# Moving eight modulation matrix products out of the QKV stage, and reworking the normalization of the attention readout, in an adaLN + linear attention + GEGLU block

## The chip, the cores and the metric

The kernel runs on one core of a Trainium2 chip. The metric is the device time of one execution in microseconds (us); lower is better. A core has a matrix engine (TensorE, "PE" in the profile; "PEld" is its weight load), a vector engine (VectorE, "DVE"), a scalar engine (ScalarE, "ACT"), GpSimd ("POOL") and a queue engine that issues DMAs (SyncE, "SP"). TensorE writes its results to tiles in a memory called PSUM. A tile of 128x512 float32 is called one bank here; a tile of 128x1024, such as `k_ps` below, is counted as two. The operands and all other tiles on the core are in a second memory, SBUF.

TensorE's clock is granted by hardware: the profile shows it as a share of full speed (over the whole execution 0.970 in the kernel before). A kernel of one core has no second die to compare with, so a run counts as fast unless it is over 1.5% above the fastest of the same kernel.

## The reference, cut to what matters

```python
# x [1, 2048, 1024], wqkv [1024, 3072], wo [1024, 1024], c [1, 1024], w_mod [1024, 6144]
# w_gate, w_up [1024, 3584], w_down [3584, 1024]; all bf16; 32 heads of 32
mod = silu(c) @ w_mod                       # six vectors of 1024: sa, ca, ga, sb, cb, gb
h = layernorm(x) * (1 + ca) + sa
q, k, v = split_heads(h @ wqkv)
phi(t) = where(t > 0, t + 1, exp(t)) + 1e-6
kv  = phi(k)^T v          (per head, 32x32)
den = phi(q) . sum_s phi(k) + 1e-6
num = phi(q) kv
x = x + ga * ((num / den) @ wo)             # linear attention
h = layernorm(x) * (1 + cb) + sb
x = x + gb * ((gelu(h @ w_gate) * (h @ w_up)) @ w_down)
```

## The kernel before

The 6144 columns of `w_mod` are treated as 12 blocks of 512. One block costs a 1 MB load, 8 matmuls of 128x512, a copy, and for four of the six vectors 4 transposes. Blocks 0 to 3 (`sa`, `ca`) are needed before the first q; the other eight only after the attention. Before the change those eight sit inside the QKV loop, one after each group of q, because TensorE has work to hide them under:

```python
    def mod_block(blk, scratch, apsum, small):
        ...
        wmb = scratch[blk % 2]
        nc.sync.dma_start(out=wmb, in_=w_mod_v[:, :, blk * NCH:(blk + 1) * NCH])
        ps = apsum.tile([P, NCH], FP32, name="mod_ps", tag="modps")
        for kt in range(KD):
            nc.tensor.matmul(ps[:], lhsT=silu_bc[:, kt, :], rhs=wmb[:, kt, :],
                             start=(kt == 0), stop=(kt == KD - 1))
        # ... evict; for sa, ca, sb, cb also 4 transposes ("mod_pst") and copies ...

    # QKV stage, for each of 4 blocks tb of 512 tokens:
                for g in range(G):
                    ps = cps_q.tile([P, NCH], FP32, name="q_ps")
                    # ... 8 matmuls, phi ...
                    if tb < 2:
                        for _ in range(a2_per_g):
                            if a2_blocks:
                                mod_block(a2_blocks.pop(0), scratch_A2, apsum2, small2)
                # ... last tb: load wo, multiply it by ga_bc on VectorE ...
                for tt in range(4):
                    psk = cps_kv.tile([P, D], FP32, name="k_ps")     # two banks
                    psv = cps_kv.tile([P, D], FP32, name="v_ps")     # two banks
                    # ... 16 + 16 matmuls, phi on k, copy of v ...
```

After QKV come `kv` (128 matmuls of 128x129) and the denominators `den` (32 matmuls). The reciprocal `rbf` has one row for each head and block of tokens (4 x 32 = 128 rows). To divide `num` by it, the 32 rows of the block of tokens are spread over 128 partitions by a matmul with a 0/1 matrix `esel4`, which uses 32 rows of the array:

```python
        for tb in range(TB):
            for g in range(G):
                psn = c4ps.tile([P, NCH], FP32, name="num_ps")
                nc.tensor.matmul(psn[:], lhsT=kvbd[:, g, :], rhs=pqT[:, g, tb * NCH:(tb + 1) * NCH],
                                 start=True, stop=True)
                pse = c4ps.tile([P, NCH], FP32, name="rexp_ps")
                nc.tensor.matmul(pse[:], lhsT=esel4[tb * H:(tb + 1) * H, g, :], rhs=rbf[tb * H:(tb + 1) * H, :],
                                 start=True, stop=True, tile_position=(tb * H, 0))
                rexp = c4w.tile([P, NCH], BF16, name="rexp")
                nc.scalar.activation(out=rexp[:], in_=pse[:], func=ACT.Identity)
                nc.vector.tensor_tensor(out=oT[:, g, tb * NCH:(tb + 1) * NCH], in0=psn[:], in1=rexp[:],
                                        op=ALU.mult)
```

Then the output projection with the second layernorm (`att_ps`, the normalized `h2t`, 128 transposes `ln_pt`, evicted to `HTbuf` by ScalarE), and the FFN: gate `g_ps`, up `u_ps`, down `d_ps`, 896 matmuls each. `gb` is applied by multiplying `w_down` with `gb_bc` as it arrives, 28 pieces of 128x1024.

Of the kernel before, what the change touches and what calls it, by code (L numbers as in the profile page):

```python
# [12 lines left out]
P = 128  # L13
# [6 lines left out]
def kernel(  # L20
# [41 lines left out]
    nc.vector.memset(eps_den[:], 1e-6)  # L62
    sa_col = consts.tile([P, KD], FP32, name="sa_col")
# [7 lines left out]
    HTbuf = longp.tile([P, max(KD * S, 2 * KD * NCH)], BF16, name="HTbuf")  # L71
# [3 lines left out]
    PKbuf = longp.tile([P, max(T * D, 8 * D + 2 * KD * NCH)], BF16, name="PKbuf")  # L75
# [20 lines left out]
    def mod_scratch(buf, base):  # L96
        return [buf[:, base + i * KD * NCH: base + (i + 1) * KD * NCH].rearrange("p (k n) -> p k n", k=KD)
                for i in range(2)]
    scratch_A1 = mod_scratch(HTbuf, 0)
    scratch_A2 = mod_scratch(PKbuf, 8 * D)  # L100

# [7 lines left out]
    def mod_block(blk, scratch, apsum, small):  # L109
        vec = (blk * NCH) // D  # L110
        off = (blk * NCH) % D
        wmb = scratch[blk % 2]
        nc.sync.dma_start(out=wmb, in_=w_mod_v[:, :, blk * NCH:(blk + 1) * NCH])
        ps = apsum.tile([P, NCH], FP32, name="mod_ps", tag="modps")
        for kt in range(KD):
            nc.tensor.matmul(ps[:], lhsT=silu_bc[:, kt, :], rhs=wmb[:, kt, :],
                             start=(kt == 0), stop=(kt == KD - 1))
        if vec in (2, 5):
            dst = ga_bc if vec == 2 else gb_bc
            nc.vector.tensor_copy(out=dst[:, off:off + NCH], in_=ps[:])  # L120
        else:
            modrow = small.tile([P, NCH], BF16, name="modrow")
            nc.scalar.activation(out=modrow[:], in_=ps[:], func=ACT.Identity)
            pst = apsum.tile([P, 4, P], BF16, name="mod_pst", tag="modps")
            for j in range(4):
                nc.tensor.transpose(out=pst[:, j, :], in_=modrow[:, j * P:(j + 1) * P],
                                    identity=ident[:])
            cidx = off // P
            if vec == 0:
                nc.vector.tensor_copy(out=sa_col[:, cidx:cidx + 4], in_=pst[:, :, 0])  # L130
            elif vec == 3:
                nc.vector.tensor_copy(out=sb_col[:, cidx:cidx + 4], in_=pst[:, :, 0])
            else:
                tmp = small.tile([P, 4], BF16, name="onep_tmp")
                nc.vector.tensor_scalar(out=tmp[:], in0=pst[:, :, 0], scalar1=1.0, scalar2=None,
                                        op0=ALU.add)
                dst = onepca_col if vec == 1 else onepcb_col
                nc.vector.tensor_copy(out=dst[:, cidx:cidx + 4], in_=tmp[:])
# [7 lines left out]
    with ExitStack() as pa:  # L146
# [5 lines left out]
        x_pre = []  # L152
        for t in range(4):
            xt = lnw.tile([P, D], BF16, name="xt")
            nc.sync.dma_start(out=xt[:], in_=x2d[t * P:(t + 1) * P, :])
            x_pre.append(xt)

        with tc.tile_pool(name="apsum1", bufs=1, space=bass.MemoryType.PSUM) as apsum1:
# [4 lines left out]
            nc.sync.dma_start(out=crow, in_=c)  # L163
            nc.scalar.activation(out=sig_row, in_=crow, func=ACT.Sigmoid)
# [7 lines left out]
            with tc.tile_pool(name="apsum1b", bufs=2, space=bass.MemoryType.PSUM) as apsum1b:  # L172
                for blk in range(0, 4):
                    mod_block(blk, scratch_A1, apsum1b, small2)
# [4 lines left out]
        with ExitStack() as pc:  # L179
            lnps = pc.enter_context(tc.tile_pool(name="lnps1", bufs=1, space=bass.MemoryType.PSUM))  # L180
            cps_q = pc.enter_context(tc.tile_pool(name="cps_q", bufs=2, space=bass.MemoryType.PSUM))
            cps_kv = pc.enter_context(tc.tile_pool(name="cps_kv", bufs=1, space=bass.MemoryType.PSUM))
            apsum2 = pc.enter_context(tc.tile_pool(name="apsum2", bufs=1, space=bass.MemoryType.PSUM))
            nc.gpsimd.memset(v_ext[:, :, :, P:P + 1], 1.0)
            a2_blocks = list(range(4, (6 * D) // NCH))
            a2_per_g = -(-len(a2_blocks) // (min(TB, 2) * G))
            for tb in range(TB):
# [28 lines left out]
# [3 lines that stand above are left out]
                        nc.tensor.matmul(ps[:], lhsT=wqkv_v[:, kt, g * P:(g + 1) * P],  # L219
                                         rhs=hT[:, kt, tb * NCH:(tb + 1) * NCH],  # L220
                                         start=(kt == 0), stop=(kt == KD - 1))
                    phi_evac(cwork, ps[:], pqT[:, g, tb * NCH:(tb + 1) * NCH], NCH, "q")
                    if tb < 2:
                        for _ in range(a2_per_g):
                            if a2_blocks:
                                mod_block(a2_blocks.pop(0), scratch_A2, apsum2, small2)
                if tb == TB - 1:
                    for kt in range(KD):
                        nc.sync.dma_start(out=wo_v[:, kt, :], in_=wo_dram[:, kt, :])
                        nc.vector.tensor_tensor(out=wo_v[:, kt, :], in0=wo_v[:, kt, :], in1=ga_bc[:], op=ALU.mult)  # L230
                for tt in range(4):
                    t = tb * 4 + tt
                    psk = cps_kv.tile([P, D], FP32, name="k_ps")
                    psv = cps_kv.tile([P, D], FP32, name="v_ps")
                    for nh in range(2):
                        for kt in range(KD):
                            nc.tensor.matmul(psk[:, nh * NCH:(nh + 1) * NCH], lhsT=hT[:, kt, t * P:(t + 1) * P],  # L237
                                             rhs=wqkv_v[:, kt, D + nh * NCH:D + (nh + 1) * NCH],
                                             start=(kt == 0), stop=(kt == KD - 1))
                    for nh in range(2):  # L240
                        for kt in range(KD):
                            nc.tensor.matmul(psv[:, nh * NCH:(nh + 1) * NCH], lhsT=hT[:, kt, t * P:(t + 1) * P],  # L242
                                             rhs=wqkv_v[:, kt, 2 * D + nh * NCH:2 * D + (nh + 1) * NCH],
                                             start=(kt == 0), stop=(kt == KD - 1))
                    phi_evac(cwork, psk[:], pk_tm[:, t, :], D, "k")
                    nc.scalar.activation(out=v_ext[:, t, :, 0:P], in_=psv[:].rearrange("p (g e) -> p g e", g=G),  # L246
                                         func=ACT.Identity)
            assert not a2_blocks

    with ExitStack() as pc3:  # L250
        c3s = pc3.enter_context(tc.tile_pool(name="c3s", bufs=1))
# [16 lines left out]
        c4w = pc3.enter_context(tc.tile_pool(name="c4w", bufs=2))  # L268
        c4d = pc3.enter_context(tc.tile_pool(name="c4d", bufs=1))
        c4psd = pc3.enter_context(tc.tile_pool(name="c4psd", bufs=1, space=bass.MemoryType.PSUM))  # L270
        c4ps = pc3.enter_context(tc.tile_pool(name="c4ps", bufs=2, space=bass.MemoryType.PSUM))
        esel4 = c4d.tile([P, G, P], BF16, name="esel4")
        nc.gpsimd.memset(esel4[:], 1.0)
        for q in range(4):
            nc.gpsimd.affine_select(
                out=esel4[q * 32:(q + 1) * 32], in_=esel4[q * 32:(q + 1) * 32],
# [3 lines left out]
        den_ps = c4psd.tile([P, NCH], FP32, name="den_ps")  # L280
        for tb in range(TB):
            for g in range(G):
                nc.tensor.matmul(den_ps[tb * H:(tb + 1) * H, :], lhsT=zfull[:, g, :],
                                 rhs=pqT[:, g, tb * NCH:(tb + 1) * NCH],
                                 start=(g == 0), stop=(g == G - 1), tile_position=(0, tb * H))
        np_used = TB * H
        rden = c4d.tile([P, NCH], FP32, name="rden")
        nc.scalar.activation(out=rden[0:np_used, :], in_=den_ps[0:np_used, :], func=ACT.Identity,
                             bias=eps_den[0:np_used, :], scale=1.0)
# [3 lines left out]
        for tb in range(TB):  # L293
            for g in range(G):
# [3 lines left out]
                pse = c4ps.tile([P, NCH], FP32, name="rexp_ps")  # L298
                nc.tensor.matmul(pse[:], lhsT=esel4[tb * H:(tb + 1) * H, g, :], rhs=rbf[tb * H:(tb + 1) * H, :],
                                 start=True, stop=True, tile_position=(tb * H, 0))  # L300
                rexp = c4w.tile([P, NCH], BF16, name="rexp")
                nc.scalar.activation(out=rexp[:], in_=pse[:], func=ACT.Identity)
                nc.vector.tensor_tensor(out=oT[:, g, tb * NCH:(tb + 1) * NCH], in0=psn[:], in1=rexp[:],  # L303
                                        op=ALU.mult)

    with ExitStack() as pd:
        lnw = pd.enter_context(tc.tile_pool(name="lnw2", bufs=6))
        lns = pd.enter_context(tc.tile_pool(name="lns2", bufs=4))
        lnps = pd.enter_context(tc.tile_pool(name="lnps2", bufs=2, space=bass.MemoryType.PSUM))
        dps = pd.enter_context(tc.tile_pool(name="dps", bufs=2, space=bass.MemoryType.PSUM))  # L310
        for tb in range(TB):
            htiles = []
            for tt in range(4):
                t = tb * 4 + tt
                xt = x1[:, t, :]
                nc.sync.dma_start(out=xt, in_=x2d[t * P:(t + 1) * P, :])
# [33 lines left out]
    with ExitStack() as pe:  # L350
        ework = pe.enter_context(tc.tile_pool(name="ework", bufs=2))
# [77 lines left out]
```

## Time and profile before

The median of 15 runs on all chips used is 957.23 us (954.23 to 959.25). The first lines are from the page of the profiled execution of the kernel before: busy time, share of the span and instructions of each engine, and the granted TensorE clock in 40 equal slices of the span, in tenths of full speed.

```profile
PE 901.7 (94%) x4245; PEld 407.6 (43%) x4328; DVE 450.9 (47%) x761; ACT 301.6 (32%) x452; POOL 24.8 (3%) x44
...
PEclk9999999999858997999999999999999999999999
```

TensorE is busy for 94% of the span, so time can only come from less matmul work, fewer waits, or a faster clock. The row of digits shows a dip, 8 5 8, a little after a quarter of the span, and a small one (7) later. The next view cuts the same execution into five stages. The columns are the stretch, its length, then busy time and number of instructions of PE, PEld, DVE, ACT and POOL, the granted clock, the mean busy share of the DMA engines, and GB/s.

```profile
0.00:28.00 28.00, 12.78 (x63) 6.03 (x65) 10.78 (x35) 9.68 (x14) 1.29 (x7) 1.00 0.94 320
28.00:236.00 208.00, 195.34 (x980) 90.53 (x999) 90.32 (x180) 105.91 (x132) 6.06 (x5) 1.00 0.26 86
236.00:289.00 53.00, 44.55 (x194) 14.01 (x194) 37.06 (x72) 20.93 (x34) 0.00 (x0) 0.66 0.38 132
289.00:367.00 78.00, 68.92 (x377) 33.45 (x383) 55.62 (x102) 26.43 (x49) 0.00 (x0) 0.92 0.18 55
367.00:956.00 589.00, 580.13 (x2634) 263.53 (x2687) 257.15 (x375) 138.62 (x226) 17.43 (x32) 0.99 0.37 106
```

They are: the start up to the first q; q, k and v with the eight blocks; kv, den and the num/rexp loop; the projection with the second layernorm; and the FFN. The third stage has a mean clock of 0.66, and 194 matmuls take 53 us there. The waits of TensorE (what it waited for, microseconds in total, times, longest) say where a cause may lie:

```profile
PE ps_silu L169 <- DVE PQbuf L165: 10.0, 1, 10.0
PE ln_pt L339 <- DVE h2t L333: 6.1, 6, 3.5
...
PE rexp_ps L299 <- DVE rbf L292: 4.1, 1, 4.1
PE mod_ps L116 <- DMA PKbuf<-in_w_mod_dram: 3.1, 3, 1.3
```

The first is the wait for `c` at the very start. The third is the wait for the reciprocal just before the num/rexp loop. The timeline of TensorE after that wait (start, duration, line, result <- operands, size; the wait before it in brackets):

```profile
254.33 1.01 PE L299 MATMUL rexp_ps<-rbf,esel 32*128 32x512 bf16 x2 [4.09 <-DVE rbf L292]
...
257.20 0.60 PE L299 MATMUL rexp_ps<-rbf,esel 32*128 32x512 bf16 x1
257.73 0.61 PE L296 MATMUL num_ps<-PQbuf,kvbd 128*128 128x512 bf16 x1
258.27 0.60 PE L299 MATMUL rexp_ps<-rbf,esel 32*128 32x512 bf16 x1
```

In the loop one matmul starts every 0.535 us, where the FFN starts one every 0.216 us, and TensorE shows as busy all the time: this is mainly a slow clock (0.50 from 254 to about 294 us), not a wait. (Half clock alone gives 0.43 us between starts.)

### The profile page before, as it was taken

Reading aid. Unit: us, or ns where it says so; the run is one execution under the profiler, and the core shown is the slowest. Engines: PE = TensorE matmul, PEld = TensorE weight load, DVE = VectorE, ACT = ScalarE, POOL = GpSimd, SP = SyncE. Lnnn points to the kernel's source line nnn. Section 1 sums busy time; section 2 is a strip of 40 time slices with the busy share of each in tenths; the row PEclk is TensorE's granted clock in tenths of the full one; section 3 lists DMA queues with packets and bytes.
Section 4 is the critical chain, followed back from the end, with each engine's and each line's share of the span. In section 5 each row is a group of like instructions: output and inputs, shape, how many; then the busy total and the mean of one; then the engine's idle time right before and its main releaser. Section 6 shows DMA issues by size and latency. Waiting matters only on the chain.

```text
span 955.3 us, 10673 instructions
## 1 busy us (share of the span) xinstructions
PE 901.7 (94%) x4245; PEld 407.6 (43%) x4328; DVE 450.9 (47%) x761; ACT 301.6 (32%) x452; POOL 24.8 (3%) x44
## 2 busy tenths in 40 slices
PE   4889999998799987999999999999999999999997
PEld 1444444444313443444444444444444444444443
DVE  4362625254766775655412655412555412655511
ACT  2564736332251434333201333201333200333200
POOL 0000000020000000000000000000000000000000
PEclk9999999999858997999999999999999999999999
DMA  9970100023700016555401455401555400545200
GB/s 308 338 256 1 45 1 23 0 89 99 255 1 0 23 33 210 155 154 148 123 23 57 136 166 142 138 23 40 153 153 156 133 23 26 168 138 163 58 23 23
DMA packets 143461, 100.33 MB, mean 105 GB/s; under 512 B 3633, under 2 KB 130609, under 8 KB 143410
## 3 DMA queue, kind: packets, MB, share of 16 engines
q1 hardware_dynamic: 141874, 95.43, 33.1%
q0 software_dynamic: 1536, 4.20, 1.2%
q8 instruction: 34, 0.56, 0.2%
q14 instruction: 17, 0.14, 0.1%
HBM read 95.42 MB, written 4.19 MB: 104 GB/s over the span
## 4 chain that ended last, share of the span: by engine, by line
issue 45%; PE 15%; POOL 1%; POOLq 0%; DVE 0%
PE g_ps L369 5%; PE u_ps L374 5%; PE d_ps L392 4%; POOL out_dram L398 1%; DVE xo L396 0%; POOLq L424 0%; POOLq L398 0%
## 5 line engine op out<-in xcount | busy, mean ns | idle before, releaser
L369 PE MATMUL g_ps<-HTbuf,Vbuf 128*128 128x512 bf16 x877 | 211.3, 381 | 2.0 <-ACT HTbuf L341 0.9
L374 PE MATMUL u_ps<-HTbuf,Vbuf 128*128 128x512 bf16 x879 | 211.3, 381 | 0.9
L392 PE MATMUL d_ps<-Wbuf,PQbuf 128*128 128x512 bf16 x754 | 170.2, 379 | 0.7
L378 ACT ACTIVATE sq<-g_ps 128x512 bf16<-128x512 f32 x112 | 66.9, 597 | 312.2 <-PE g_ps L369 252.7
L369 PEld LDWEIGHTS <-Vbuf 128*128 128x128 bf16 x896 | 88.0, 98 | 107.5 <-issue 2.7
L374 PEld LDWEIGHTS <-Vbuf 128*128 128x128 bf16 x896 | 88.0, 98 | 106.9 <-issue 2.1
L392 PEld LDWEIGHTS <-PQbuf 128*128 128x128 bf16 x896 | 87.7, 98 | 105.7
L380 DVE SCALAR_TENSOR_TENSOR wv<-sq,g_ps 128x512 bf16<-128x512 bf16 x112 | 77.0, 687 | 78.1 <-ACT sq L378 78.1
L385 DVE TENSOR_TENSOR tt<-sg,u_ps 128x512 bf16<-128x512 bf16 x112 | 77.0, 687 | 76.9 <-ACT sg L383 76.8
L396 DVE TENSOR_TENSOR xo<-d_ps,PKbuf 128x512 bf16<-128x512 f32 x32 | 22.1, 691 | 167.0 <-PE d_ps L392 167.0
L383 ACT ACTIVATE sg<-wv 128x512 bf16<-128x512 bf16 x112 | 70.5, 629 | 83.6 <-DVE wv L380 83.6
L386 DVE TENSOR_TENSOR PQbuf<-tt,g_ps 128x512 bf16<-128x512 bf16 x112 | 76.9, 686 | 3.8
L219 PE MATMUL q_ps<-HTbuf,Wbuf 128*128 128x512 bf16 x249 | 63.3, 379 | 1.8 <-DVE PQbuf L144 0.7
L237 PE MATMUL k_ps<-Wbuf,HTbuf 128*128 128x512 bf16 x251 | 62.8, 379 | 1.1 <-DVE PKbuf L144 0.7
L242 PE MATMUL v_ps<-Wbuf,HTbuf 128*128 128x512 bf16 x250 | 62.3, 379 | 1.4 <-ACT Vbuf L246 0.9
L320 PE MATMUL att_ps<-Wbuf,Vbuf 128*128 128x512 bf16 x249 | 61.3, 391 | 1.5 <-DVE Vbuf L303 1.0
L237 PEld LDWEIGHTS <-HTbuf 128*128 128x128 bf16 x256 | 25.0, 98 | 30.8 <-issue 1.1
L242 PEld LDWEIGHTS <-HTbuf 128*128 128x128 bf16 x256 | 25.0, 98 | 30.7 <-issue 1.0
L320 PEld LDWEIGHTS <-Vbuf 128*128 128x128 bf16 x256 | 24.7, 100 | 27.9 <-issue 5.4
L398 POOL DMA_DIRECT2D out_dram<-xo x32 | 17.4, 545 | 734.6 <-DVE xo L396 734.6
L219 PEld LDWEIGHTS <-Wbuf 128*128 128x128 bf16 x256 | 23.7, 98 | 25.9 <-issue 4.5
L143 DVE TENSOR_SCALAR phi_e_q<-phi_e_q 128x512 bf16<-128x512 bf16 x32 | 10.4, 324 | 49.5 <-ACT phi_e_q L142 49.5
(81 smaller groups left out, 561.6 us busy)
## 6 DMA issues: line engine op xcount, KB each, us to landing
Vbuf<-in_B_w_gate_dram SPq DMA_DIRECT2D x56, 512.0 KB, 3.7
Vbuf<-in_B_w_up_dram SPq DMA_DIRECT2D x56, 512.0 KB, 4.8
PKbuf<-in_w_mod_dram SPq DMA_DIRECT2D x8, 1024.0 KB, 6.3
Wbuf<-in_A_wqkv_dram SPq DMA_DIRECT2D x3, 2048.0 KB, 14.7
Wbuf<-in_B_w_down_dram SPq DMA_DIRECT2D x24, 256.0 KB, 5.5
xt<-in_A_x_dram SPq DMA_DIRECT2D x16, 256.0 KB, 4.2
HTbuf<-in_w_mod_dram SPq DMA_DIRECT2D x4, 1024.0 KB, 6.6
PKbuf<-in_A_x_dram SPq DMA_DIRECT2D x16, 256.0 KB, 5.5
```

What stands on the lines that cost most here:

```text
L219: nc.tensor.matmul(ps[:], lhsT=wqkv_v[:, kt, g * P:(g + 1) * P], rhs=hT[:, kt, tb * NCH:(tb + 1) * NCH], start=(kt == 0), stop=(kt == KD - 1))
L237: nc.tensor.matmul(psk[:, nh * NCH:(nh + 1) * NCH], lhsT=hT[:, kt, t * P:(t + 1) * P], rhs=wqkv_v[:, kt, D + nh * NCH:D + (nh + 1) * NCH], ...
L242: nc.tensor.matmul(psv[:, nh * NCH:(nh + 1) * NCH], lhsT=hT[:, kt, t * P:(t + 1) * P], rhs=wqkv_v[:, kt, 2 * D + nh * NCH:2 * D + (nh + 1) ...
L320: nc.tensor.matmul(ps[:, nh * NCH:(nh + 1) * NCH], lhsT=oT[:, g, t * P:(t + 1) * P], rhs=wo_v[:, g, nh * NCH:(nh + 1) * NCH], start=(g == ...
L369: nc.tensor.matmul(psg[:], lhsT=wge[:, kt, j * P:(j + 1) * P], rhs=h2T[:, kt, tb * NCH:(tb + 1) * NCH], start=(kt == 0), stop=(kt == KD - 1))
L374: nc.tensor.matmul(psu[:], lhsT=wue[:, kt, j * P:(j + 1) * P], rhs=h2T[:, kt, tb * NCH:(tb + 1) * NCH], start=(kt == 0), stop=(kt == KD - 1))
L378: nc.scalar.activation(out=sq[:], in_=psg[:], func=ACT.Square)
L380: nc.vector.scalar_tensor_tensor(out=wv[:], in0=sq[:], scalar=INV_C, in1=psg[:], op0=ALU.add, op1=ALU.mult)
L383: nc.scalar.activation(out=sg[:], in_=wv[:], func=ACT.Sigmoid, scale=SIG_SCALE)
L385: nc.vector.tensor_tensor(out=tt1[:], in0=sg[:], in1=psu[:], op=ALU.mult)
L386: nc.vector.tensor_tensor(out=gT[:, ft, :], in0=tt1[:], in1=psg[:], op=ALU.mult)
L392: nc.tensor.matmul(psd[:], lhsT=gT[:, ft, tt * P:(tt + 1) * P], rhs=wd_ft(ft)[:, nh * NCH:(nh + 1) * NCH], start=(ft == 0), stop=(ft == KF ...
```

## The change

Its intent is to take modulation work out of the QKV stage and put it where TensorE waits anyway, to keep the clock up in the num/rexp loop, and to shorten the start and the handover to the FFN. The diff, cut to its core (comments with "..." mark cuts):

```diff
 # --- start: c first, four w_mod blocks issued up front, 20 warm-up matmuls ---
             nc.sync.dma_start(out=crow, in_=c)
+            # ... x tiles loaded here, after c ...
+            for b4 in (0, 2, 1, 3):
+                nc.sync.dma_start(out=wmod_sc[:, :, b4 * NCH:(b4 + 1) * NCH],
+                                  in_=w_mod_v[:, :, b4 * NCH:(b4 + 1) * NCH])
+            warm_ps = apsum1.tile([P, NCH], FP32, name="warm_ps")
+            for i in range(20):
+                nc.tensor.matmul(warm_ps[:], lhsT=ident[:], rhs=zeros[:], start=True, stop=True)
 # --- QKV: one PSUM bank more for q, four one-bank tiles for k and v, no modulation ---
-            cps_q = pc.enter_context(tc.tile_pool(name="cps_q", bufs=2, ...))
+            cps_q = pc.enter_context(tc.tile_pool(name="cps_q", bufs=3, ...))
-                    if tb < 2:
-                        # ... mod_block(a2_blocks.pop(0), scratch_A2, apsum2, small2)
-                        # (and wo * ga_bc on VectorE, moved behind QKV)
-                    psk = cps_kv.tile([P, D], FP32, name="k_ps")
-                    psv = cps_kv.tile([P, D], FP32, name="v_ps")
+                    for part, base in (("k", D), ("v", 2 * D)):
+                        for nh in range(2):
+                            ps = cps_kv.tile([P, NCH], FP32, name=f"{part}{nh}_ps")
+                            # ... 8 matmuls, then phi (k) or copy (v) of 512 columns
 # --- behind QKV: two loads of 4 MB, blocks 4 to 7, wo * ga; x1 preloaded ---
+        nc.sync.dma_start(out=wmod_sc, in_=w_mod_v[:, :, 2 * D:4 * D])
+        wmod_sc2 = wqkv_v[:, :, D:3 * D]
+        nc.sync.dma_start(out=wmod_sc2, in_=w_mod_v[:, :, 4 * D:6 * D])
+        mod_blocks([4, 5, 6, 7], 2 * D, apsum2, small2)
 # --- rexp on all 128 rows: esel4 [P, TB, G, P], zero outside the block's 32 rows ---
+        weave = mod_steps([8, 9, 10, 11], 4 * D, apsum2, small2, wmod_sc2)
-                nc.tensor.matmul(pse[:], lhsT=esel4[tb * H:(tb + 1) * H, g, :], rhs=rbf[tb * H:(tb + 1) * H, :],
-                                 start=True, stop=True, tile_position=(tb * H, 0))
+            nc.tensor.matmul(pse_t[i][:], lhsT=esel4[:, tb, g, :], rhs=rbf[:], start=True, stop=True)
 # --- in the loop (fixed order on TensorE): rexp of pair i+1, num of pair i, then
+                if i >= 4:
+                    next(weave, None)          # one modulation matmul of blocks 8 to 11
+                    if i % 4 == 0:
+                        next(weave, None)
 # --- projection: pools ---
-        lnw = ... bufs=6;  lnps = ... bufs=2;  dps = ... bufs=2
+        lnw = ... bufs=7;  dps = ... bufs=3;   lnps = ... bufs=2
 # --- FFN: 12 of the 28 w_down scalings on GpSimd; pools with reuse_waits="tile" ---
-                        nc.vector.tensor_tensor(out=wd_ft(ft), in0=wd_ft(ft), in1=gb_bc[:], op=ALU.mult)
+                        eng = nc.gpsimd if (ft >= KFW or ft % 3 == 0) else nc.vector
+                        eng.tensor_tensor(out=wd_ft(ft), in0=wd_ft(ft), in1=gb_bc[:], op=ALU.mult)
```

## The prediction

> **What bounds it now.** TensorE: PE is 94% busy (page, first part), but the stage windows differ:
>
> | stage (us of the span) | length | PE busy | granted clock |
> |---|---|---|---|
> | start, to first q, 0-28 | 28 | 12.8 | 1.00 |
> | q, k, v and 8 modulation blocks, 28-236 | 208 | 195.3 | 1.00 |
> | kv, den, num/rexp, 236-289 | 53 | 44.5 | 0.66 |
> | output projection, second layernorm, 289-367 | 78 | 68.9 | 0.92 |
> | FFN, 367-955 | 588 | 580 | 0.99 |
>
> A warm 128x512 matmul starts every 0.216 us (FFN timeline). In the num/rexp loop one starts every 0.535 us: the clock falls to 0.50 while PE waits 4.1 us for the reciprocal (waits view: rexp_ps on rbf) and stays there from 254 to 294 us although PE shows as busy. [...]
>
> **What changes, and what it is worth**
>
> 1. Start: c is loaded first, all four modulation blocks are issued before wqkv. The DMA bound: 1 MB x + 4 MB w_mod + 2 MB wq at the 0.31-0.36 MB/us of this stretch is about 22 us. First q near 23: -5.
> 2. Eight blocks leave the qkv stage: 64 matmuls x 0.216 = 14 us, 16 transposes 1 us, and their stalls (mod_ps on DMA 3.1 us). 768 x 0.216 + transposes is 173 us; layernorm stalls of 1.6 us per block stay, since lnps keeps one buffer. Split k/v PSUM helps little. 208 becomes about 181: -27.
> 3. kv to num: adds 64 modulation matmuls (14 us at full clock) and 16 transposes. 8 MB of w_mod can only load after the last v matmul, 12 us per 4 MB; kv (9 us) and den (4.5 us) cover the first half, 24 modulation matmuls fill the reciprocal gap. Full-row rexp and weaving should keep PE warm. VectorE then limits: 8 wo scalings (0.6 each) come before 32 evictions at 0.645 each. 53 becomes about 49: -4, with 14 us more work.
> 4. Projection: no cold start (-3), third PSUM buffer, x1 preloaded; but 16 w_down scalings now land here on VectorE (10 us), which becomes about as full as PE. 67 to about 63. The handover (last projection matmul 355.8, first gate matmul 367.1) shrinks to about 5, bounded by the first gate load: together -10.
> 5. FFN: same 2,688 matmuls: +2.
>
> 23 + 181 + 49 + 68 + 590 = 911 span, +2 (now 957.2 against 955.3): **913 us, range 901 to 930**. Faster by over 2%: 0.95; within 2%: 0.04; slower: 0.01.
>
> **What would show it.** Clock near 1.0 throughout num/rexp, matmuls every 0.22 us there with PE waiting on DVE or on DMA into Wbuf; last v matmul near 204 us; a PE wait of 1-3 us on w_mod DMA after den; VectorE above 85% in the projection; FFN still about 588.
>
> **What would make it wrong.** The num loop staying at half clock: 100 matmuls x 0.43 would add about 20 us (to about 933). w_mod arriving later than 15 us after the last v matmul. VectorE stuck on w_down before the first projection eviction.

The inference: the 32-row rexp matmuls keep the clock from coming back. It was drawn from the clock of 0.50 from 254 to 294 us, while TensorE shows as busy. On it rests item 3 (full-row rexp keeps the clock up), an estimate at that time, which the runs below test. 23 + 181 + 49 + 68 + 590 = 911 us of span, and 2 more make 913 us.

## The result, and the profile after

The kernel after takes 918.03 us (median of 8 runs, 915.28 to 918.68). The ratio to the kernel before is 0.9585, with a 95% interval of 0.9573 to 0.9597. Ratios here and below are the mean time of one kernel's fast runs over that of the other's fast runs of the same rounds, so they are not quite the ratio of the medians quoted. Where two experiments ran on different chips, only their ratios to the kernel before are compared.

The page of the kernel after, the same lines as before:

```profile
PE 881.3 (96%) x4264; PEld 407.6 (44%) x4348; DVE 447.0 (49%) x782; ACT 301.0 (33%) x482; POOL 56.3 (6%) x60
...
PEclk9999999999999999999999999999999999999999
```

The dip of the clock is gone, and TensorE is busy 20 us less with 19 instructions more: in the loop before, at half clock, a matmul is shown with 0.60 us, in the loop after with 0.38. The stages of the kernel after, with the same columns:

```profile
0.00:26.50 26.50, 17.57 (x91) 8.32 (x93) 11.01 (x37) 9.30 (x14) 1.13 (x7) 1.00 0.96 323
26.50:207.40 180.90, 176.20 (x867) 81.40 (x882) 80.75 (x189) 102.00 (x153) 1.50 (x1) 1.00 0.13 46
207.40:256.10 48.70, 43.61 (x303) 23.15 (x305) 40.94 (x77) 23.92 (x41) 10.90 (x9) 1.00 0.87 322
256.10:324.70 68.60, 63.05 (x351) 30.13 (x358) 59.77 (x108) 21.66 (x40) 4.38 (x2) 1.00 0.11 37
324.70:917.00 592.30, 580.86 (x2659) 264.60 (x2714) 254.54 (x373) 144.11 (x234) 38.38 (x42) 0.99 0.38 110
```

| stage | before | predicted | after |
|---|---|---|---|
| start, to first q | 28 | 23 | 26.5 |
| q, k, v | 208 | 181 | 180.9 |
| kv, den, modulation, num/rexp | 53 | 49 | 48.7 |
| projection and handover to the first gate matmul | 78 | 68 | 68.6 |
| FFN to the end | 588 | 590 | 592.2 |

The third row is the remarkable one: it now holds 303 matmuls in place of 194, and is 4 us shorter, because its clock is 1.00 in place of 0.66. The loop of the kernel after in the timeline, with the same columns as the loop above:

```profile
236.17 0.38 PE L319 MATMUL num_ps<-PQbuf,kvbd 128*128 128x512 bf16 x1
236.38 0.38 PE L114 MATMUL mod_ps<-Wbuf,silu_bc 128*128 128x512 bf16 x1
236.60 0.38 PE L312 MATMUL rexp_ps<-rbf,esel 128*128 128x512 bf16 x1
236.82 0.38 PE L319 MATMUL num_ps<-PQbuf,kvbd 128*128 128x512 bf16 x1
```

A matmul starts every 0.216 us here, and rexp has become 128*128 on a 128x512 operand. The longest waits of TensorE in the kernel after:

```profile
PE ps_silu L178 <- DVE PQbuf L174: 6.4, 1, 6.4
PE ln_pt L364 <- DVE h2t L358: 3.9, 5, 1.9
...
PE u_ps L400 <- DVE tt L411: 2.9, 1, 2.9
...
PE att_ps L345 <- DVE gb_bc L119: 1.6, 1, 1.6
```

The wait for `rbf` is gone from the list, the 3.5 us wait for `h2t` at the handover too. A new one is there: 2.9 us of `u_ps` on `tt`, at 334 us, just after the first gate matmuls; this wait explains part of why the FFN became 4 us longer. The timeline around it:

```profile
331.48 1.48 ACT L366 ACTIVATE HTbuf<-ln_pt,sb_col,onepcb_col 128x512 bf16<-128x512 bf16 x2
...
332.81 1.13 ACT L404 ACTIVATE sq<-g_ps 128x512 bf16<-128x512 f32 x2
...
336.65 1.66 PE L400 MATMUL u_ps<-HTbuf,Vbuf 128*128 128x512 bf16 x5 [2.87 <-DVE tt L411]
```

With the new pools the first gate and up matmuls no longer wait for the last transposes. They fill their two PSUM buffers, but ScalarE evicts the last layernorm tiles first (to 332.96), then `sq`, a 1.28 us table load and `sg`; only then does VectorE's `tt` free `u_ps`. The clock falls to 0.50 once more for a few microseconds (338 to 340) after this idle time of 2.87 us.

### The profile page after: what moved, and what is told of

The parts are those of the page before. It is cut to its first block, busy times and chain, and to the rows that moved or that the text cites. A ratio compares the mean times of both kernels' runs of the same rounds, so it can differ in the third digit from the quotient of the medians.

```text
span 916.9 us, 10763 instructions
## 1 busy us (share of the span) xinstructions
PE 881.3 (96%) x4264; PEld 407.6 (44%) x4348; DVE 447.0 (49%) x782; ACT 301.0 (33%) x482; POOL 56.3 (6%) x60
## 4 chain that ended last, share of the span: by engine, by line
PE 53%; issue 34%; DVE 7%; ACT 3%; POOL 1%; DMA 1%; another core or an unknown queue 0%; POOLq 0%; SPq 0%; ACTq 0%; DVEq 0%
PE g_ps L395 10%; PE u_ps L400 10%; PE d_ps L418 8%; PE k_ps L237 6%; PE q_ps L224 6%; PE v_ps L237 6%; ACT HTbuf L366 2%; PE att_ps L345 2%; PE mod_ps L114 1%; POOL out_dram L424 1%; PE ln_pt L216 1%; DVE stats L351 1%; DVE PKbuf L348 1%; PE warm_ps L172 1%; DVE h2t L358 1%
## 5 line engine op out<-in xcount | busy, mean ns | idle before, releaser
L345 PE MATMUL att_ps<-Wbuf,Vbuf 128*128 128x512 bf16 x249 | 58.8, 379 | 1.9 <-DVE gb_bc L119 1.6
L224 PE MATMUL q_ps<-HTbuf,Wbuf 128*128 128x512 bf16 x247 | 59.6, 379 | 0.4
L237 PE MATMUL v_ps<-Wbuf,HTbuf 128*128 128x512 bf16 x250 | 57.4, 379 | 0.3
L418 PE MATMUL d_ps<-Vbuf,PQbuf 128*128 128x512 bf16 x124 | 32.0, 379 | 0.1
L147 DVE TENSOR_SCALAR phi_e_k<-phi_e_k 128x512 bf16<-128x512 bf16 x32 | 9.2, 291 | 43.5 <-ACT phi_e_k L146 43.5
```

Of the source, the lines that this page charges most:

```text
L224: nc.tensor.matmul(ps[:], lhsT=wqkv_v[:, kt, g * P:(g + 1) * P], rhs=hT[:, kt, tb * NCH:(tb + 1) * NCH], start=(kt == 0), stop=(kt == KD - 1))
L237: nc.tensor.matmul(ps[:], lhsT=hT[:, kt, t * P:(t + 1) * P], rhs=wqkv_v[:, kt, base + nh * NCH:base + (nh + 1) * NCH], start=(kt == 0), st ...
L345: nc.tensor.matmul(ps[:, nh * NCH:(nh + 1) * NCH], lhsT=oT[:, g, t * P:(t + 1) * P], rhs=wo_v[:, g, nh * NCH:(nh + 1) * NCH], start=(g == ...
L418: nc.tensor.matmul(psd[:], lhsT=gT[:, ft, tt * P:(tt + 1) * P], rhs=wd_ft(ft)[:, nh * NCH:(nh + 1) * NCH], start=(ft == 0), stop=(ft == KF ...
```

## The experiments

Two theories stood at the start for the largest effect, the clock of the num/rexp loop. **A**: the 32-row matmuls themselves keep the clock at 0.50, however busy TensorE looks. **B**: the 4 us wait for the reciprocal starts the low state, and filling that gap is what helps. A third, **C**, was that weaving modulation matmuls into the loop keeps the clock up. The other experiments take one further part of the change back, or try to improve on it. All twelve kernels gave correct results.

### Full-row rexp alone, in the kernel before

```diff
-        esel4 = c4d.tile([P, G, P], BF16, name="esel4")          # ones by affine_select, 32 rows used
+        esel4 = c4d.tile([P, TB, G, P], BF16, name="esel4")      # zero outside the block's 32 rows
-                nc.tensor.matmul(pse[:], lhsT=esel4[tb * H:(tb + 1) * H, g, :], rhs=rbf[tb * H:(tb + 1) * H, :],
-                                 start=True, stop=True, tile_position=(tb * H, 0))
+                nc.tensor.matmul(pse[:], lhsT=esel4[:, tb, g, :], rhs=rbf[:], start=True, stop=True)
```

> The kernel before, with one part of the change: the rexp matmul contracts over all 128 rows (zero-padded selector) instead of 32. The 4 us wait for the reciprocal stays. Theory A[...]: the clock falls to 0.50 in the wait, then recovers some 4 to 6 us into the num/rexp loop; the loop shrinks from 33.7 us to 22-25 us (then bound by 32 VectorE evictions at 0.645 us), the projection starts warm, total about 944 to 948 us. Rival B (the wait alone, or the loop's duty, decides): the clock stays at 0.50 through the loop, matmuls start every 0.43 us, the loop takes about 28 us, total 950 to 953.

Measured: 946.91 us (946.38 to 948.69), ratio 0.9906 (0.9885 to 0.9927). The wait for `rbf` is still 4.1 us. The windows of its loop, with the columns as above:

```profile
256.00:260.00 4.00, 1.31 (x3) 0.36 (x3) 2.53 (x3) 0.95 (x2) 0.00 (x0) 0.76 1.05 396
260.00:264.00 4.00, 4.00 (x10) 1.21 (x9) 3.12 (x5) 2.58 (x6) 0.00 (x0) 0.50 0.21 76
264.00:268.00 4.00, 3.38 (x12) 1.09 (x11) 3.67 (x6) 3.15 (x6) 0.00 (x0) 0.89 0.00 0
268.00:272.00 4.00, 3.29 (x13) 1.00 (x12) 3.88 (x7) 3.36 (x6) 0.00 (x0) 1.00 0.00 0
```

The gap still brings the clock to 0.50, but it is back at full speed some 6 us into the loop and stays there to the loop's end. From the last v matmul to the first projection matmul it takes 47.1 us in place of 54.0, and the projection, which no longer starts cold, 64.6 in place of 67.2: together 9.5 us, which is the gain within what runs differ. So the 32-row form is what holds the clock down, shown alone and in fast runs: padding this matmul with zero rows is worth a quarter of what the whole change gives.

The same trace shows a second thing, earlier, while `kv` is computed with full rows:

```profile
236.00:240.00 4.00, 2.03 (x23) 1.36 (x21) 4.00 (x9) 1.03 (x1) 2.74 (x1) 1.00 0.90 304
240.00:244.00 4.00, 3.10 (x30) 3.00 (x31) 3.94 (x13) 0.00 (x0) 3.82 (x4) 0.62 1.01 362
```

In this stage TensorE waits three times for VectorE (`kv_ps` on `kvbd`), 2.5 us in all and at most 1.1 us at once, with only short matmuls of 129 columns between; it is busy 2.03 us of the four from 236 to 240, and the clock is at 0.50 from 241 to about 244.4 us. VectorE's small operations take up to 2.26 us here while GpSimd fills the larger `esel4`. (The kernel before, with waits of 1.00, 0.89, 0.30 and 0.69 us in the same place, kept its clock.) So here, with pauses, the clock fell with all 128 rows in use, and the 9.5 us above already include this loss.

### The gap filled, 32-row rexp kept, in the kernel before

```diff
+        fill_ps = c4psd.tile([P, NCH], FP32, name="fill_ps")
+        with tc.manual_schedule(engines={PE}):       # fixed order on TensorE
+            for i in range(26):
+                nc.tensor.matmul(fill_ps[:], lhsT=kvbd[:, i % G, :], rhs=pqT[:, i % G, 0:NCH], ...)
+            # ... then the num/rexp loop as before, in the order num, rexp
```

> The kernel before, with 26 unused full-size matmuls (5.6 us) put into the wait for the reciprocal; the 32-row rexp stays. Rival B (the wait is the cause): the clock stays at 1.0, the loop becomes VectorE-bound at about 21 us, total about 942 to 946. Theory A[...]: the clock starts at 1.0 but falls to 0.50 within about 4 to 8 us of the loop's start, and stays; total 950 to 957.

Measured: 964.79 us (963.50 to 966.81), ratio 1.0092 (1.0068 to 1.0115). The windows of its loop:

```profile
256.00:260.00 4.00, 2.99 (x11) 0.84 (x9) 1.36 (x3) 1.84 (x4) 0.00 (x0) 1.00 0.66 248
260.00:264.00 4.00, 3.00 (x7) 0.59 (x6) 2.64 (x4) 1.80 (x4) 0.00 (x0) 0.66 0.01 2
264.00:268.00 4.00, 3.34 (x7) 0.60 (x6) 2.08 (x3) 2.18 (x4) 0.00 (x0) 0.50 0.02 4
```

The loop starts at full clock, and loses it after about 5 us, with no gap before it and with no wait in it longer than 0.9 us. It stays at 0.50 to about 302 us. So B falls: the gap is not needed for the low state, and filling it does not prevent it. (The total missed what either theory expected, for the reason given below.)

It does not prove all of A, though, because the 32-row form changes two things. The array has fewer rows at work, and the matmuls stand further apart. In the first microseconds of this loop, still at full clock, a matmul that follows one of the other shape starts 0.32 us after it, not 0.216; at half clock it is 0.535 us against the 0.43 of the full-row loop above. The weight loads show where the 0.1 us go: here the load of 0.10 us starts together with its own matmul (the first of rexp both at 256.6 us; in the kernel before 257.19 and 257.20 us), in the loop of the kernel after one whole matmul earlier (235.95 and 236.17 us). The engine's busy row hides the gap, since a matmul's modelled end reaches over the gap. In the `kv` stage of the full-row run above the clock fell among full-row matmuls with short pauses (three, 2.5 us in all); so "short pauses" is a rival to "few rows". The next experiment has two comparisons that bear on it.

A flaw of this experiment: the fixed order num before rexp made TensorE wait for VectorE in every second pair (6.0 us in 15 waits), which is part of why the kernel became slower, so its total time is not a measure of the gap, and it too thins out the matmuls.

### 32-row rexp in the kernel after

```diff
-            nc.tensor.matmul(pse_t[i][:], lhsT=esel4[:, tb, g, :], rhs=rbf[:], start=True, stop=True)
+            nc.tensor.matmul(pse_t[i][:], lhsT=esel4[tb * H:(tb + 1) * H, tb, g, :], rhs=rbf[tb * H:(tb + 1) * H, :],
+                             start=True, stop=True, tile_position=(tb * H, 0))
```

> The changed kernel with the 32-row rexp put back; weave, order and gap filling stay. Theory A with weaving: [...]the clock stays at 1.0, and only the unhidden weight loads of mixed row groups cost, 0.1 us each, so 0 to +6 us (918 to 924). If row tiling itself takes the clock down whatever stands around it: +15 us or more (933 and up).

Measured: 942.80, 942.98, 923.45 and 943.29 us. By the 1.5% rule three of these are slow runs and have no ratio, so this experiment supports A but does not carry it alone. In the profiled one of the three, the low clock is not spread over the execution, as it is in the slow run of the kernel with all w_down scalings on VectorE below (about 0.75 from start to end). It begins in the loop and ends a few microseconds into the projection:

```profile
232.00:236.00 4.00, 3.14 (x12) 0.84 (x11) 3.48 (x7) 2.12 (x4) 0.00 (x0) 0.77 1.05 386
236.00:240.00 4.00, 4.00 (x9) 0.68 (x9) 1.67 (x3) 1.28 (x3) 0.00 (x0) 0.50 1.05 388
...
280.00:284.00 4.00, 4.00 (x10) 1.32 (x9) 4.00 (x7) 0.00 (x0) 0.00 (x0) 0.50 0.14 51
```

The mean clock of the span tells the same: 0.971 in the three, 0.994 in the one of 923.45 us (no trace of that one). My expectation, C, missed in three runs of four: in those three weaving did not keep the clock up with rexp on 32 rows, although two of three matmuls in the loop are full. From the last v matmul to the first projection matmul it took 72.6 us in place of 48.5. This is the loss that the prediction named as its main risk.

The comparison: from 231.14 to 234.35 us, just before its clock fell, this run started 6 matmuls of 512 columns and 4 transposes, 3 of the 6 with 32 rows. The kernel after started the same number, 6 and 4, from 231.75 to 234.88 us, all with full rows and with the same wait of 0.86 us in it, and kept its clock. At the same density of starts the clock fell with the 32-row form and held with full rows. A second pair points the same way: at half clock, the full-row run above started 13 matmuls from 258.37 to 264.59 us, one per 0.48 us, and then had its clock back; this run started about one per 0.50 us, every third with 32 rows, and stayed at 0.50 for the 43 us to the end of its loop. This speaks for few rows in this loop; but elsewhere, with pauses, the clock fell with full rows (`kv` in the full-row run, the start without warm-ups below). How much each of the two counts stays open, and one of the traces compared is of a slow run. What is shown is that the 32-row form, with what it brings, is the cause in this loop.

### Blocks 8 to 11 issued before the loop in the program, in the kernel after

```diff
-        weave = mod_steps([8, 9, 10, 11], 4 * D, apsum2, small2, wmod_sc2)
+        with tc.manual_schedule(engines={PE}):
+            for _ in mod_steps([8, 9, 10, 11], 4 * D, apsum2, small2, wmod_sc2):
+                pass
+        weave = iter(())
```

> The changed kernel with modulation blocks 8 to 11 in one piece (32 matmuls, 7 us, plus their transposes) ahead of the rest of the num/rexp loop instead of woven into it. Theory (full-row rexp keeps the clock, weaving only hides 7 us of TensorE work under VectorE's evictions): the clock stays at 1.0, the loop's evictions start later, +4 to +7 us (922 to 925). Rival (the woven matmuls are needed to keep the clock): it falls to 0.50 in the loop, +10 us or more (928 and up).

Measured: 919.39 us (917.19 to 921.55), ratio 0.9602 (0.9575 to 0.9630), clock 1.00 throughout the loop. The trace shows that the edit did not give one piece ahead of the loop: the blocks ran as pieces of 8, 8 and 16 matmuls between 234.6 and 243.7 us, after the loop had begun and with num and rexp between them. From 244 to 257 us the loop then ran without any woven matmul, two starts every 0.63 us, and the clock stayed at 1.00: weaving is not needed for the clock. The stage of kv to num took 51.6 us in place of 48.5; the projection then took 2 us less, which is not due to this edit (see gb on the output, below). The intervals of this kernel and of the kernel after overlap. Weaving is worth at most a few microseconds, less than expected.

### The old PSUM tiles of q, k and v, in the kernel after

```diff
-            cps_q = ... bufs=3
+            cps_q = ... bufs=2
-                            ps = cps_kv.tile([P, NCH], FP32, name=f"{part}{nh}_ps")   # four tiles of one bank
+                    psk = cps_kv.tile([P, D], FP32, name="k_ps")
+                    psv = cps_kv.tile([P, D], FP32, name="v_ps")                      # two tiles of two banks
```

> The changed kernel with the old k and v PSUM tiles (two banks each, evicted whole) and two q banks. Theory (the qkv stage got shorter because 64 modulation matmuls and their stalls left it): the stage stays at 181 to 184 us, total +0 to +3 us (918 to 921). Rival (the finer PSUM tiles gave a large part of the 27 us): +8 us or more (926 and up).

Measured: 921.61 us (920.52 to 922.23), ratio 0.9624 (0.9602 to 0.9647). From the first q to the last v matmul it takes 185.0 us, against 181.1 in the kernel after and 206.7 before. So the finer tiles of k and v and the third bank of q, which this edit takes back together, give about 4 of the 26 us of this stage, a little more than the theory's 0 to 3 and far from the rival's 8. The moved blocks, by subtraction, give about 22. Their bare work is 64 matmuls of 0.216 us plus about 1 us of transposes, near 15 us; the remaining 7 are put down to waits that they brought into the stage, of which the waits view of the kernel before shows 3.1 us on their loads; the rest was not itemized.

### No warm-up matmuls, in the kernel after

```diff
-            warm_ps = apsum1.tile([P, NCH], FP32, name="warm_ps")
-            for i in range(20):
-                nc.tensor.matmul(warm_ps[:], lhsT=ident[:], rhs=zeros[:], start=True, stop=True)
```

> The changed kernel without its 20 warm-up matmuls. They ran from 7.4 to 14.5 us and the first modulation matmul began right after them, although its inputs (silu_bc at 8.7 us; first block of w_mod about 10.3 us) were there earlier. Theory (the warm-ups themselves delay the start): the first modulation matmul moves to 9-11 us, cold, and the first q matmul from 26.5 to about 23-25, total 2 to 4 us less. Rival (the start is bound by the arrival of w_mod and wq): first q stays at 26 or later, total within 1 us of the changed kernel, or slower by the cold clock.

Measured: 919.09 us (917.66 to 920.46), ratio 0.9612 (0.9590 to 0.9633). The timeline of TensorE in this kernel, the first modulation block and the first q:

```profile
9.88 3.57 PE L114 MATMUL mod_ps<-HTbuf,silu_bc 128*128 128x512 bf16 x8 [2.25 <-DMA HTbuf<-in_w_mod_dram]
...
26.63 0.59 PE L221 MATMUL q_ps<-HTbuf,Wbuf 128*128 128x512 bf16 x2
```

Without warm-ups the first block starts at 9.9 us, cold (8 matmuls in 3.57 us). With them it starts at 14.5 us, warm (8 in 1.89 us, 0.216 us apart), because the warm-ups occupy TensorE until 14.7 us. The chain of the four blocks ends at 23.6 us without and at 26.0 us with warm-ups. And still the first q starts at 26.6 us without and 26.5 us with them: the load of the q weights, issued at 10.3 us in the kernel after, took 14.4 us to land (24.7 us), and without warm-ups the scheduler also placed more transposes ahead of the first q. Without warm-ups the clock also fell to 0.50 once more, from about 27.3 to 30.8 us, after four waits of 0.27 to 0.87 us for ScalarE among full-row matmuls (22.7 to 26.4 us). Within what the intervals resolve, the warm-ups neither help nor hurt; to shorten the start, both the load and the transposes would have to come earlier. Which of the two binds was not separated. A warning for reading such traces: the clock column shows 1.00 from 12 to 15 us in the kernel before and from 8 to 13 us in the kernel after, although matmuls start 0.43 us apart there. In the first microseconds of these executions only the distance between starts shows the low state.

### The old pools of the projection, in the kernel after

```diff
-        lnw = ... bufs=7;  dps = ... bufs=3;  lnps = ... bufs=2
+        lnw = ... bufs=6;  lnps = ... bufs=2; dps = ... bufs=2
```

> The changed kernel with the projection's old PSUM pools (two att_ps, transposes' pool first, six h2t). Then all last transposes stand before the first gate matmul again. Theory (handover gain comes from gate matmuls running ahead of the last transposes): last projection matmul to first gate matmul goes from 2.5 us back to about 8 to 11 us, total +4 to +8 us (922 to 926). Rival (the handover is bound by the gate weights' DMA either way): within 2 us.

Measured: 918.65 us (918.03 to 919.45), ratio 0.9597 (0.9570 to 0.9623): no difference from the kernel after that the intervals would show. The handover is the old one:

```profile
PE ln_pt L364 <- DVE h2t L358: 5.6, 5, 3.5
```

From the last projection matmul to the first gate matmul it takes 10.4 us, against 2.4 in the kernel after (11.1 before). But from there to the end it takes 587.1 us against 592.2, and the projection 64.3 against 66.2. So the handover did become 8 us shorter, and 5 of these were given back in the FFN: the 26 transposes that were passed over come later (1.6 us), and the `u_ps` wait costs 2.9 us. The matmuls at half clock are no part of the difference: both kernels lose some 1.7 us by them (14 matmuls in 4.7 us from 336.65 us in the kernel after, the first 8 gate matmuls in 3.35 us here). The 1.9 us in the projection are not the pools' doing (see gb on the output, below). That leaves at most 3 us of gain, which these runs do not resolve. What the early gate matmuls gained was for the most part a different place for the same waiting.

### Every second of the last eight layernorm evictions on VectorE

This tries to shorten the new wait. The theory was that the eight evictions on ScalarE cause it; the rival, that it comes from elsewhere, for example from ScalarE's table load.

```diff
+                if tb == TB - 1 and kt % 2 == 1:
+                    nc.vector.tensor_scalar(out=hT[...], in0=pt[:], scalar1=onepcb_col[:, kt:kt + 1],
+                                            scalar2=sb_col[:, kt:kt + 1], op0=ALU.mult, op1=ALU.add)
+                else:
                     nc.scalar.activation(out=hT[...], in_=pt[:], ...)
```

> The changed kernel with every second of the last eight h2T evictions (ln_pt to HTbuf) on VectorE, which is idle then, instead of all eight on ScalarE. In the changed kernel ScalarE does them from 327.5 to 332.9 us, so the first gate psum is squared only at 332.8, and u_ps waits 2.9 us for it, after which the clock falls to 0.50 for about 4 us. Theory: the wait shrinks to under 1 us and the clock stays up: 3 to 5 us less than the changed kernel (913 to 915). Rival (the wait comes from elsewhere, e.g. ScalarE's table load): under 1 us less.

Measured: 915.96 us (915.45 to 916.61), ratio 0.9564 (0.9551 to 0.9577), against 0.9585 for the kernel after; the intervals still touch. The wait did become shorter:

```profile
PE u_ps L405 <- DVE tt L416: 1.9, 1, 1.9
```

One microsecond less wait, after which the clock stayed at 1.00, and by the ratios some 2 us less in all: less than expected, and not resolved. (The kernel without reuse_waits, below, ran in the same rounds and should equal the kernel after; its mean is 916.93 us, against 916.00 here.) After the evictions the chain `sq`, `wv`, a 1.28 us table load, `sg`, `tt` remains, and TensorE still waits for its end.

### All w_down scalings on VectorE

```diff
-                        eng = nc.gpsimd if (ft >= KFW or ft % 3 == 0) else nc.vector
+                        eng = nc.vector
```

> The changed kernel with all w_down scalings on VectorE as before (GpSimd took 12 of 28, at 2.1 us each). Theory (they are off the critical path on either engine): within 2 us of the changed kernel. Rival 1 (VectorE is needed at the start of the FFN, where the 2.9 us wait of u_ps on tt stands): +2 to +5 us. Rival 2 (GpSimd slows VectorE[...]): 1 to 3 us less.

Measured: 919.21, 918.83 and 918.99 us in the fast runs, ratio 0.9598 (0.9573 to 0.9624), and 1173.47 us in one slow run. The slow run had a clock of about 0.75 from start to end; the profile fell on it, so there is no trace of a fast run. Within what the intervals resolve, giving 12 scalings to GpSimd does nothing.

### gb on the output in place of on w_down

```diff
-                        eng.tensor_tensor(out=wd_ft(ft), in0=wd_ft(ft), in1=gb_bc[:], op=ALU.mult)   # 28 of 128x1024
+                    nc.vector.tensor_tensor(out=xs[:], in0=psd[:], in1=gb_bc[:, nh * NCH:(nh + 1) * NCH], op=ALU.mult)
+                    nc.vector.tensor_tensor(out=xo[:], in0=xs[:], in1=x1[:, t, nh * NCH:(nh + 1) * NCH], op=ALU.add)
```

> The changed kernel without the 28 w_down scalings by gb; gb is multiplied at the output instead (one more VectorE operation per output tile, in a stage where VectorE is under 15% busy). It takes 16 scalings, about 10 us, off VectorE in the projection, and 12 off GpSimd. Theory (VectorE holds up the projection): projection 66.2 us to 62-63 us, its first eviction not behind seven scalings, total 3 to 4 us less, minus about 0.7 us at the very end (914 to 916). Rival (TensorE holds up the projection): within 1.5 us of the changed kernel.

Measured: 916.88 us (915.96 to 918.69), ratio 0.9575 (0.9562 to 0.9589), an interval that overlaps that of the kernel after. VectorE is busy 48.2 of the 64.5 us of the projection in place of 57.8 of 66.2, and TensorE is busy 62.8 of them: the projection is bound by TensorE. The 1.7 us between 66.2 and 64.5 are not the edit's doing. In the traces of six other kernels that keep the scalings (old pools, no weaving, old PSUM tiles, no warm-ups, shared evictions, no reuse_waits) the projection takes 64.3 to 64.4 us, so taking 10 us off VectorE brings nothing that can be seen. In the profiled run of the kernel after, the difference can be seen as one event, a VectorE operation that took 2.42 us in place of 0.54 while GpSimd worked, in the timeline at 289 us:

```profile
288.82 2.42 DVE L358 TENSOR_SCALAR h2t<-PKbuf,mv,rstd 128x1024 bf16<-128x1024 bf16 x1
288.84 4.38 POOL L390 TENSOR_TENSOR Vbuf<-Vbuf,gb_bc 128x1024 bf16<-128x1024 bf16 x2 [70.05 <-DMA Vbuf<-in_B_w_down_dram]
291.29 0.23 PE L364 MATMUL ln_pt<-ident,h2t 128*128 128x128 bf16 x1 [1.89 <-DVE h2t L358]
```

In this trace the same operation has a median of 0.54 us, and took 2.42 us while the GpSimd operation ran. In the traces of three other kernels with the same GpSimd work (old PSUM tiles, old pools, no reuse_waits) its longest is 0.85 us, and in three without it (the kernel before, all scalings on VectorE, gb on the output) 0.55 us. So the size is not the same from trace to trace; what sets it was not tested.

### Both improvements together

```diff
+        # the two edits above: evictions shared with VectorE, gb on the output
```

> Both of the above, the eviction split and gb at the output. If their effects add: 909 to 912 us, faster than both kernels. If they are the same wait seen twice: 913 to 915.

Measured: 915.95 us (913.02 to 916.19), ratio 0.9556 (0.9541 to 0.9572). This is the best ratio of all, 0.3% below that of the kernel after, and its interval ends where that one begins (0.9572 and 0.9573). The expected 909 to 912 us were missed because each gain alone was smaller than expected; in the ratios the two add (0.9585 - 0.0021 - 0.0010 = 0.9554, measured 0.9556), but the intervals are too wide to tell. An improvement on the kernel after is not shown either: the next kernel, which should equal it and ran in the same rounds, has a mean of 916.93 us against 915.28 here, and its interval overlaps this one.

### Without reuse_waits in the FFN pools

```diff
-        ework = pe.enter_context(tc.tile_pool(name="ework", bufs=2, reuse_waits="tile"))   # and three more pools
+        ework = pe.enter_context(tc.tile_pool(name="ework", bufs=2))
```

> The changed kernel without reuse_waits in the four FFN pools. Instructions and order on TensorE are the same, only some waits of ScalarE and VectorE differ. Expected: within 1 us of the changed kernel, FFN still 592 us. If finer waits mattered: over 2 us slower.

Measured: 915.87 us (915.53 to 918.78), ratio 0.9577 (0.9561 to 0.9593). It is the same as the kernel after; this setting is not part of the gain. It also shows how far the stages wander without cause: its start is 0.9 us shorter than in the kernel after, though nothing in it was changed, so single stage times below some 2 us should not be read.

## Why the prediction was right, point by point

The prediction of 913 us (901 to 930) was 5 us below the measured 918.03, inside its range, and the direction was right.

- **What bounds it.** Right: TensorE, with a clock problem in one stage. The inference that the 32-row rexp matmuls keep the clock from coming back was the one thing that the trace before could not show. The full-row run shows that the 32-row form is the cause, and the filled-gap run that the gap is not needed. That it is the rows, and not the larger distance between such matmuls, is likely for this loop and not shown.
- **Start, -5.** This step failed: it became 1.5 us. The estimate divided 7 MB by the rate of that stretch, about 22 us. The load of the q weights landed at 24.7 us: 323 GB/s over 26.5 us is 8.6 MB, so other loads took their part of the rate (worked out, not tested). And four blocks in a chain, started only when the warm-ups were done, ended at 26.0 us. The term was mis-sized by 3.5 us, most of the miss in the total.
- **q, k, v, -27.** Right in sum (208 to 180.9; predicted 181). One remark in it was wrong: "Split k/v PSUM helps little." Together with the third bank of q it gives about 4 us. Layernorm waits were lower than the 1.6 us for each block that were left in the estimate (the longest is 1.1 us), and this is where the two errors met: the exact sum is in part luck.
- **kv to num, -4.** Right: 48.7 us against 49 predicted. Clock 1.00, matmuls every 0.216 us. The expected wait of 1 to 3 us on the w_mod load did not occur; the largest wait before the loop is 1.1 us, on VectorE. The risk named, a loop at half clock, "about 20 us (to about 933)", was measured in the kernel with 32 rows: 24 us in the stage, 942.9 us in the three runs that fell into it.
- **Projection, -10.** Right in sum (68.6 against 68), not in its parts: 63 + 5 was predicted, 66.2 + 2.4 measured (64.3 for the first term in six other traces); that the errors cancel is luck. VectorE at 87% is as predicted, but the experiment with gb on the output shows that this costs nothing that can be seen. The handover is shorter than predicted, since gate matmuls pass the last transposes.
- **FFN, +2.** Mis-sized: it became 4 us longer. The prediction saw the shorter handover as a gain and not as work put off. The transposes, the evictions and the first activation chain have to happen all the same, and now do so in the first microseconds of the FFN.

Adding the measured differences from the first q, last v, first projection matmul and first gate matmul in the two traces gives 1.5 (start) + 25.7 (q, k, v) + 5.5 (kv to num) + 9.7 (projection and handover) - 3.9 (FFN), which is, but for rounding, the whole difference of the spans, 955.3 - 916.9 = 38.4 us. The 5.5 hide two large terms: the modulation work added to this stage, some 15 us, and the low clock taken out of it. The order of the two matters: with 32-row rexp the moved work lands in a loop at half clock, and in three runs of four 25 of the 39 us are lost again.

Left open: how much few rows and how much pauses count when the clock falls; why the kernel with 32 rows and weaving kept its clock in one run of four; which of load and transposes binds the start; and whether the 1.28 us table load in front of the first `sg` could be moved ahead of the handover.

## What to carry to other kernels

A TensorE that shows 100% busy may still run at half clock (here 0.50 for 40 us, a matmul every 0.535 us in place of 0.216): read the granted clock and the distance between matmul starts, and where few-row matmuls alternate with full ones in a loop, try padding them with zero rows before filling gaps (here padding alone gave 0.9906 of the time before, filling the gap alone 1.0092, and the padded ones even stood closer together). Before moving work into a stage, make sure of that stage's clock, since the moved work costs double at half clock (0.43 us between starts of full-row matmuls in place of 0.216). And a handover that becomes shorter is only a gain if the work it skips disappears; measure to the end of the kernel, not to the next stage's first instruction.

## What these traces showed of the hardware

- A loop alternating 128-row and 32-row matmuls lost the clock 5 us in with no wait over 0.9 us (the filled-gap run), and in the kernel before it stayed at 0.50 for 40 us while TensorE showed as busy nearly all the time; with all rows in use, zero or not, the clock was back after 6 us (the full-row run). The denominator's matmuls, with 128 rows and 32 columns, 5.8 us of work in the kernel after, ran at 1.00.
- A matmul after one of the other shape (128 and 32 rows) started after 0.32 us at full clock (the filled-gap run) and 0.535 us at half (the kernel before), against 0.216 us (the kernel after) and 0.43 us (the full-row run) among full ones.
- In the kernel after, 2.9 us of idling (333.8, a modelled end, to 336.7 us) were followed by 0.50 from 338 to 340 us; 1.9 us in the kernel with shared evictions were not; among full-row matmuls with three waits of at most 1.1 us, 2.5 us in all, the clock fell to 0.50 for 3.4 us (`kv` in the full-row run).
- The kernel with all w_down scalings on VectorE ran one whole execution at 0.754 (1173.47 us against 919); no run explains it.
- A 128x4 VectorE operation took 0.22 us in the kernel before, between 0.66 and 1.28 us in the kernel after while GpSimd filled a matrix, and 2.26 us at most in the full-row run; a 128x1024 one 0.54 us, and 2.42 us once.
- The bf16 multiplication of 128x1024 took 2.12 us on GpSimd and 0.68 us on VectorE in the kernel after, 3.1 times.
